# The first nine attention units as one flat list, and batch 1's values by casting DMA

## The chip, the cores and the metric

The kernel runs on one core of a Trainium2 chip. Its engines are TensorE (PE in the profile; PEld is its weight loads), VectorE (DVE), ScalarE (ACT), GpSimd (POOL) and SyncE (SP, which here only issues DMAs). Each takes its instructions in the order of the program and waits on semaphores for the others. The metric is the device time of one execution, in microseconds (us).

## The reference

Two stages, the second fed by the first:

```python
# attention: B=8 batches, H=8 heads, 512 local and 32 global positions, head size 64
k_all = concat([k_g, k_l]);  v_all = concat([v_g, v_l])
out_g = softmax(scale * q_g @ k_all.T) @ v_all               # global queries see everything
s_ll  = where(|i - j| <= 32, scale * q_l @ k_l.T, -1e9)      # local queries: a window
out_l = softmax(concat([scale * q_l @ k_g.T, s_ll])) @ v_all # and the global keys
x = concat([out_g, out_l]) reshaped to (4352, 512)
# mixture of E=8 experts, F=1024
P = exp(x @ w_gate - max);  8 times: P /= rows' sums; P /= columns' sums; P *= N / E
out = sum over e of P[:, e] * (relu(x @ w1[e]) @ w2[e])
```

## The kernel before, in words

**Units.** Attention is cut into 32 units: unit n is two heads (pair n mod 4) of batch n // 4. A unit goes through these steps, each a function:

- st_A (L266): TensorE transposes keys and queries (fp16, cast before by POOL, cast_qk) into PSUM; VectorE copies the keys to kTe, ACT the queries to the block-diagonal qbd (two copies).
- st_B0 and st_B (L314, L287), in three parts: scores of eight blocks of 64 queries against a window of 128 keys and the 32 global keys; row minima or maxima on VectorE, exp with its sums on ACT into Pu. Batch 0 uses st_B0 (mask added by TensorE), the others st_B (mask added by VectorE).
- st_N (L343): reciprocals and scaling of Pu on VectorE, the global part Pl on POOL.
- st_D1, st_D2 (L355, L363): transposes of Pu and Pl and their copies out of PSUM, pw on VectorE, pg on ACT.
- st_E (L371): weights times values into po, copied to xT, the first layer's input. The first layer of batch 0 needs st_E of units 0 to 3.

The global queries have steps of their own, st_G0, st_G1, st_GN, st_G2 and st_G3, for a half batch each; transpose_g (L205) makes their keys kgT and queries qgT from what cast_g cast.

**Values.** st_E reads values of a batch in two tilings, va and vb, and global ones in vgz. From batch 2 on, load_v (L174) fetches them with POOL-issued DMAs that cast fp32 to fp16; SP then copies va to vb (move_vb) and fills vgz (load_vz). Batches 0 and 1 are loaded raw in fp32 (load_vrow), cast by POOL to vsr and rearranged by TensorE with a 0/1 matrix: select_v (L151), four 128x512 matmuls into one PSUM tile and a copy, for each 128-row piece. Batch 0 takes eight such products, batch 1 five, and two DMAs from ACT's queue fill the rest of its vb.

**Fillers.** The first layer of experts 0 to 3 (p_l1, L461) is mixed into attention. One block is four 128x512 matmuls and a ReLU out of PSUM by ACT or VectorE; f1("a") or f1("v") (L490) issues the next one, in the order expert 0, 1, 2, 3 for batch 0 (eight blocks each), then batch 1, and so on. A block of a batch is let through only from slot 4 x batch + 5 on. Expert weights come by load_w1e (L477), a casting DMA that POOL issues into a software queue. What stays over of the fillers is done beside the Sinkhorn iterations after attention, and then the other experts follow.

**Order.** Nothing is scheduled by a tool: the order of calls is the order on each engine. Units 0 to 2 are emitted by a loop (L525 to L558), the next steps by straight code up to L585, units 4 on by the loop at L588, with special cases for its first rounds. From its round 9 the loop has a steady form: one unit and seven or eight fillers a round, 30 in four rounds. Fillers begin in round 4, two there and seven in each of rounds 5 to 8. DMAs on SP's queue (q, k, raw values, global keys and queries, value moves, results) are issued in the same program order.

PSUM pools: mm and sc two buffers each, po one, tr two. kTe has eight buffers, Pu, pw and pg two.

Of the kernel before, what the change touches and what calls it, by code (L numbers as in the profile page):

```python
# [23 lines left out]
def kernel(  # L24
# [67 lines left out]
    with tc.tile_pool(name="att_c", bufs=1) as att_c, \  # L92
# [42 lines left out]
        vraw = {}  # L135

        def load_vrow(b):
            shape = [P, H, NJ, Dh]
            f = vraw[b] = (hpool.tile(shape, FP32, tag="hT", name="vraw") if b else
                           wpool.tile(shape, FP32, tag="w2e", name="vraw", bufs=1))  # L140
            for g in range(2):
                nc.sync.dma_start(out=f[:, 4 * g : 4 * g + 4].rearrange("p h s d -> p h (s d)"),
                                  in_=v_l[b, 4 * g : 4 * g + 4].rearrange("h (p s) d -> p h (s d)", s=NJ))

        def cast_vrow(b, gs=(0, 1)):
            f = vraw[b]
            for g in gs:
                h = slice(4 * g, 4 * g + 4)
                nc.gpsimd.tensor_copy(out=vsr[:, :, h, :], in_=f[:, h].rearrange("p h s d -> p s h d"))

        def select_v(b, t, js, po=()):  # L151
            for j in js:
                c0 = P * j + HB * t
                pool, tag = (ps_po, "po") if j in po else (ps_mm, "mm")
                pv = pool.tile([P, D], FP32, tag=tag, name="pv")
                for so in range(NJ):
                    nc.tensor.matmul(pv, zsel[:, so, c0 : c0 + P], vsr[:, so], start=(so == 0), stop=(so == NJ - 1))
                cp = nc.vector.tensor_copy if j % 2 == 0 else nc.scalar.copy
                cp(out=vab[b % 2][t][:, j], in_=pv.rearrange("p (h d) -> p h d", h=H))
# [70 lines left out]
        load_vrow(0)  # L230
# [35 lines left out]
        def st_A(n):  # L266
# [11 lines left out]
            for a in range(2):  # L278
                r = slice(HB * a, HB * (a + 1))
                o = qb[r, :, HB * a : HB * (a + 1)].rearrange("p i (q s) -> p i q s", s=NJ)  # L280
                i = pq[r, 1, :].rearrange("p (s i q) -> p i q s", s=NJ, i=NHB)
                if b == 0:
                    nc.scalar.mul(o, i, -scale)
                else:
                    nc.scalar.copy(out=o, in_=i)  # L285
# [69 lines left out]
        def st_D1(n):  # L355
# [5 lines left out]
            nc.vector.tensor_copy(out=d["pw"], in_=ptw)  # L361

        def st_D2(n):  # L363
# [5 lines left out]
            nc.scalar.copy(out=d["pg"], in_=pt)  # L369

        def st_E(n):  # L371
# [13 lines left out]
            cp = nc.vector.tensor_copy if HP <= n < 2 * HP else nc.scalar.copy  # L385
            cp(out=xT[b][:, hp, :], in_=po)
# [138 lines left out]
        for s in range(3):  # L525
            for part in range(3):
                st_B0(s, part)
            if s >= 1:
                st_D1(s - 1)
                st_D2(s - 1)  # L530
            if s == 0:
                cast_vrow(0)
                cast_qk(0, 1, gq)
                load_qk(1, 0, (nc.sync, nc.sync))
                load_g(k_g, kgf)
                load_w1e(0)
                nc.vector.memset(qbd[1], 0.0)
            elif s == 1:
                load_vrow(1)
                load_qk(1, 1, (nc.sync, nc.sync))  # L540
                load_vg(1)
                init_vgz(vgz[1], nc.gpsimd)
                load_vz(1)
                qgf = hpool.tile([P, H, NJ * Dh], FP32, tag="hT", name="qgf")
                load_g(q_g, qgf)
            else:
                load_w1e(1)
                nc.gpsimd.dma_start(out=wg_sb, in_=moe_w_gate.rearrange("(dko dki) e -> dki dko e", dki=P))
                cast_qk(1, 0, gq)
                gk0 = cast_g(kgf, 0)  # L550
            pad_k((kTe[s + 2],))
            st_A(s + 1)
            if s < 2:
                select_v(0, s, (0, 1), (0,))
                st_N(s, 0, 6)
                if s == 0:
                    select_v(0, 0, (2, 3), (3,))
                st_N(s, 6, NHB)  # L558
        select_v(0, 1, (2, 3))
        st_B0(3, 0)  # L560
        st_B0(3, 1)
        st_E(0)
        st_A(4)
        st_B0(3, 2)
        st_N(2, 0, 6)
        st_N(2, 6, NHB)
        cast_vrow(1, (0,))
        pad_k(kTe[5:7])
        nc.vector.memset(mask[:, :, KW:SW], 0.0)
        nc.vector.tensor_scalar(out=mask[:, :, 0:KW], in0=m16, scalar1=-HUGE * 8.0, scalar2=None, op0=ALU.mult)  # L570
        st_E(1)
        st_D1(2)
        st_D2(2)
        transpose_g(gk0, 0, kgT)
        st_N(3, 0, 6)
        st_N(3, 6, NHB)
        st_B(4, 0)
        st_E(2)
        cast_vrow(1, (1,))
        load_w1e(2)  # L580
        for t in qgbd:
            nc.vector.memset(t, 0.0)
        st_D1(3)
        st_B(4, 1)
        st_D2(3)  # L585
        gat = {s: s - 5 for s in range(5, 9)}
        gat.update({2 * j + 1: j for j in range(4, NU // 2)})
        for s in range(HP, NU + 1):  # L588
# [8 lines left out]
            if s == HP:  # L597
                st_A(s + 1)
                st_B(s, 2)
                st_E(s - 1)  # L600
                st_N(s, 0, 6)
                st_N(s, 6, NHB)
                select_v(1, 0, (0, 1))
                st_B(s + 1, 0)
                select_v(1, 0, (2, 3))
                select_v(1, 1, (NJ - 1,))
                slot = s + 1
                va, vb = vab[1]
                nc.scalar.dma_start(out=vb[0:HB, 0 : NJ - 1], in_=va[HB:P, 0 : NJ - 1])
                nc.scalar.dma_start(out=vb[HB:P, 0 : NJ - 1], in_=va[0:HB, 1:NJ])  # L610
                cast_qk(1, 1, gq)
                gcast = [(cast_g(x[0], x[1]), x) for x in ((kgf, 1, kgT), (qgf, 0, qgT), (qgf, 1, qgT))]
                load_w1e(3)
            else:
                if HP + 1 < s <= 2 * HP:
                    st_B(s, 0)
                if s > 2 * HP:
                    f1("a")
                st_D1(s - 1)
                if g23:  # L620
                    st_GN(*gp)
            if g1 and s > HP + 1:
                st_G0(*gn)
            f1("a" if s > 2 * HP else "aa")
            if s > HP:
                st_D2(s - 1)
            if 2 * HP < s < NU:
                st_B(s, 0)
            if g23 and s <= 2 * HP:
                st_G2(*gp)  # L630
            if HP < s < NU:
                st_B(s, 1)
            if s > HP:
                f1("vv" if g23 else "va")
            if g23 and s > 2 * HP:
                st_G2(*gp)
            if HP < s < NU - 1:
                st_A(s + 1)
            if HP < s < NU:
                st_B(s, 2)  # L640
            if s > HP:
                f1("v")
                st_E(s - 1)
# [4 lines left out]
            if g23:  # L648
                st_G3(*gp)
# [589 lines left out]
```

## Time and profile before

| | before |
|---|---|
| median of 3 runs | 1031.53 us (1030.57 to 1031.58) |
| the profiled execution | 1031.69 us, its span 1029.9 us |
| first filler block starts | 46.17 us |
| round 9 starts | 91.83 us |
| granted TensorE clock, mean | 0.997 |

In the table of stretches, a row holds the stretch in us from the span's start, its length, and for PE, PEld, DVE, ACT and POOL the busy time with the number of instructions in brackets; then the granted TensorE clock, the mean busy share of the 16 DMA engines, and GB/s. In a row of a group of instructions stand line, engine, operation, output<-inputs, shapes and count; after the first bar the busy time in us and the mean ns of one; after the second the idle time just before them and what ended it. A row of the timeline begins with its start and its length in us. "us min/median/max" at a DMA is from its issue to its landing; the rows named q0 are the software queue's packets, MB and share of 16 engines.

### The profile page before, as it was taken

What the parts mean: (1) busy time and instruction counts of PE and PEld (TensorE: products, weight loads), DVE (VectorE), ACT (ScalarE), POOL (GpSimd) and SP (SyncE); (2) the same over time, 40 slices, a digit from 0 to 9 for tenths busy, and PEclk for the clock granted to TensorE, in tenths of its full rate; (3) what the DMA queues carried; (4) which work ended last, traced back from release to release, by engine and by line L of the source; (5) the groups of instructions that cost most, each with busy time, mean ns of one, the idle gap of its engine ahead of it and who ended that gap; (6) DMA issues with size and microseconds to landing.
All of it is one profiled execution on the core that took longest, in us unless ns stands there. A gap on an engine that the chain in (4) does not pass through costs nothing.

```text
span 1029.9 us, 23231 instructions
## 1 busy us (share of the span) xinstructions
PE 1004.5 (98%) x9286; PEld 741.1 (72%) x9286; DVE 891.1 (87%) x1740; ACT 528.7 (51%) x1328; POOL 172.2 (17%) x265
## 2 busy tenths in 40 slices
PE   7899999999999999999999999999999999999998
PEld 4555555555555466777778878878878878888887
DVE  8688877877775768999879999999999999999995
ACT  7767888888886674222223434333333333433431
POOL 7341423414403003021110000000000000000000
PEclk9899999999999999999999999999999999999999
DMA  9896698989946989957646656665755746746750
GB/s 269 192 221 194 135 277 203 218 238 205 222 144 173 285 283 308 310 182 279 235 159 232 200 188 230 200 191 193 224 186 184 240 175 206 232 173 194 220 195 27
DMA packets 103180, 216.87 MB, mean 211 GB/s; under 512 B 34384, under 2 KB 67616, under 8 KB 92576
## 3 DMA queue, kind: packets, MB, share of 16 engines
q1 hardware_dynamic: 52576, 165.38, 46.4%
q0 software_dynamic: 47888, 40.39, 21.9%
q10 hardware_dynamic: 2608, 9.64, 2.4%
q8 instruction: 72, 1.18, 0.5%
q14 instruction: 36, 0.29, 0.1%
HBM read 174.41 MB, written 59.12 MB: 227 GB/s over the span
## 4 chain that ended last, share of the span: by engine, by line
PE 83%; DVE 8%; ACT 6%; issue 2%; DMA 1%; SPq 0%; POOL 0%; ACTq 0%; DVEq 0%
PE m L931 27%; PE ph L468 18%; PE ph L820 11%; PE pm L931 10%; PE pf L838 10%; ACT Pu L311 2%; DVE Pu L348 2%; DVE h L693 1%; ACT qbd L285 1%; PE ptw L359 1%; PE pt L275 1%; DVE s L693 1%; PE po L380 1%; ACT hT L471 1%; DMA vraw<-in_v_l_dram 1%
## 5 line engine op out<-in xcount | busy, mean ns | idle before, releaser
L468 PE MATMUL ph<-xT,w1e 128*128 128x512 f16 (+1 forms) x1152 | 259.7, 367 | 2.7 <-ACT hT L471 1.3
L931 PEld LDWEIGHTS <-h 128*128 128x128 f16 x2160 | 209.9, 98 | 35.7 <-DVE h L693 2.2
L931 PE MATMUL m<-w2c,s 128*128 128x256 f16 x1620 | 199.9, 273 | 0.0
L931 PEld LDWEIGHTS <-s 128*128 128x128 f16 x1620 | 158.5, 98 | 26.6
L468 PEld LDWEIGHTS <-w1e 128*128 128x128 f16 x1152 | 105.1, 98 | 98.0 <-issue 8.8
L822 ACT ACTIVATE h<-ph 128x512 f16<-128x512 f32 (+1 forms) x144 | 79.1, 550 | 150.2 <-PE ph L820 140.9
L693 DVE TENSOR_TENSOR h<-h,pb 128x2048 f16<-128x2048 f16 (+2 forms) x66 | 154.9, 2347 | 0.5 <-DMA h<-hd 0.5
L845 ACT ACTIVATE h<-pf 128x512 f16<-128x512 f32 x144 | 82.1, 596 | 123.4 <-PE pf L838 112.0
L693 DVE TENSOR_TENSOR s<-h 128x1024 f16<-128x1024 f16 (+2 forms) x178 | 127.5, 757 | 17.4 <-ACT h L822 12.8
L931 PE MATMUL m<-w2c,h 128*128 128x256 f16 x1080 | 138.2, 273 | 0.0
L820 PE MATMUL ph<-xs,w1s 128*128 128x512 f16 (+1 forms) x576 | 127.3, 355 | 0.0
L931 PE MATMUL pm<-w2c,h 128*128 128x256 f16 x1080 | 124.8, 273 | 0.5
L471 ACT ACTIVATE hT<-ph 128x512 f16<-128x512 f32 (+1 forms) x188 | 102.1, 559 | 38.1 <-PE ph L468 36.0
L838 PEld LDWEIGHTS <-w1q 128*128 128x128 f16 x1008 | 98.6, 98 | 11.4
L311 ACT ACTIVATE Pu<-ms,mx 128x160 f16<-128x160 f32 x224 | 93.3, 424 | 4.6 <-DVE mx L308 3.9
L473 DVE TENSOR_SCALAR hT<-ph 128x512 f16<-128x512 f32 x100 | 67.7, 686 | 28.2 <-PE ph L468 28.0
L693 DVE TENSOR_TENSOR h<-h 128x1024 f16<-128x1024 f16 (+1 forms) x178 | 91.5, 555 | 0.4
L693 DVE TENSOR_TENSOR xs<-xg,pb 128x1024 f16<-128x1024 f16 (+2 forms) x48 | 79.7, 1661 | 7.9 <-DMA hd<-hT 7.8
L820 PEld LDWEIGHTS <-w1s 128*128 128x128 f16 x576 | 56.4, 98 | 37.7
L838 PE MATMUL pf<-xs,w1q 128*128 128x256 f16 x576 | 80.5, 273 | 0.0
L308 DVE CUSTOM_DVE_ANT_0 ms<-sc,mask 128x160 f32<-128x160 f32 x224 | 59.2, 318 | 9.6 <-PE sc L303 9.5
L838 PE MATMUL pf<-t,w1q 128*128 128x256 f16 x432 | 64.8, 273 | 0.0
(168 smaller groups left out, 1217.5 us busy)
## 6 DMA issues: line engine op xcount, KB each, us to landing
h<-hd SPq DMA_DIRECT2D x32, 1024.0 KB
w1q<-w1c SPq DMA_DIRECT2D x36, 896.0 KB
hd<-hT SPq DMA_DIRECT2D x26, 1024.0 KB
w1s<-w1d SPq DMA_DIRECT2D x18, 1024.0 KB
pb<-pd SPq DMA_DIRECT2D x64, 256.0 KB
w2c<-in_moe_w_dram POOLq DMA_DIRECT2D x16, 512.0 KB, 22.3
out_dram<-o POOLq DMA_DIRECT2D x8, 1024.0 KB, 4.7
f<-in_q_l_dram SPq DMA_DIRECT2D x15, 512.0 KB
```

The lines of the kernel that those rows point to most:

```text
L308: nc.vector.tensor_tensor_reduce(out=ms[:, ii, :], in0=sc[:, SW * ii : SW * (ii + 1)], in1=mask[:, mi, :], scale=-scale, scalar=BIG, op0=A ...
L311: nc.scalar.activation(out=d["Pu"][:, i, :], in_=ms[:, ii, :], func=AF.Exp, scale=-1.0, bias=d["mx"][:, i : i + 1], accum_out=d["sm"][:, i ...
L348: nc.vector.tensor_tensor(out=d["Pu"][:, i0:i1, 0:KW], in0=d["Pu"][:, i0:i1, 0:KW], in1=d["rs"][:, i0:i1].unsqueeze(2).to_broadcast([P, i1 ...
L468: nc.tensor.matmul(ph[:, 0:n], wts[e][:, dk, P * fm : P * (fm + 1)], xT[m][:, dk, :], start=(dk == 0), stop=(dk == DP - 1))
L471: nc.scalar.activation(out=hT[:, fm, 0:n], in_=ph[:, 0:n], func=AF.Relu)
L473: nc.vector.tensor_scalar(out=hT[:, fm, 0:n], in0=ph[:, 0:n], scalar1=0.0, scalar2=None, op0=ALU.max)
L693: nc.vector.tensor_tensor(out=out, in0=in0, in1=in1, op=op)
L820: nc.tensor.matmul(ph[:, 0:n], w1s[i][:, dk, P * fm : P * (fm + 1)], xss[i][:, dk, 0:n], start=(dk == 0), stop=(dk == DP - 1))
L822: nc.scalar.activation(out=hs[i][:, fm, 0:n], in_=ph[:, 0:n], func=AF.Relu)
L838: nc.tensor.matmul(bank[:, 256 * c : 256 * (c + 1)], self.w[:, self.sta[q], k, P * c : P * (c + 1)], self.mov[q][:, k], start=(first and c ...
L845: nc.scalar.activation(out=self.h[:, k : k + 2, 256 * c : 256 * (c + 1)], in_=bank.rearrange("p (k t) -> p k t", k=2), func=AF.Relu)
L931: nc.tensor.matmul(pm[:, HD * t : HD * (t + 1)], lhs[0][:, k, lhs[1] + P * t : lhs[1] + P * (t + 1)], w[:, k, q - 1, :], start=(k == 0 and ...
```

## The change

The loop over units 0 to 2, the straight code and the loop's rounds 4 to 8 are replaced by one flat list of calls for units 0 to 8; the loop begins at round 9, in its steady form. In the list the parts of different units are interleaved singly, and fillers stand as single blocks between other steps; there are 30 of them, as before.

- Batch 1's values: load_vrow, cast_vrow and the five select_v of batch 1 go; load_v(1) is called instead, with a memset of 32 rows of va that it leaves unwritten. Batch 0 keeps its eight products, in another order.
- st_A, st_D1, st_D2, st_E and select_v take the engine of their copies as an argument ("a" ACT, "v" VectorE). So pw of units 1, 2, 4 and 5 is copied by ACT, qbd of unit 5 by VectorE, pg of units 5 and 7 by VectorE, xT of unit 1 and 6 by VectorE and of the other units by ACT.
- The expert weights are issued in the order 1, 2, 0 ahead of the fillers and 3 after the eighteenth of them; before, 0, 1, 2, 3.
- Loads of q, k and global keys and queries, their casts, paddings and clears stand at other places of the list.

```diff
-        def load_vrow(b):
-            shape = [P, H, NJ, Dh]
-            f = vraw[b] = (hpool.tile(shape, FP32, tag="hT", name="vraw") if b else
-                           wpool.tile(shape, FP32, tag="w2e", name="vraw", bufs=1))
+        vraw = wpool.tile([P, H, NJ, Dh], FP32, tag="w2e", name="vraw", bufs=1)
...
-        def select_v(b, t, js, po=()):
...
-                cp = nc.vector.tensor_copy if j % 2 == 0 else nc.scalar.copy
...
+        def copy(eng, out, in_):
+            (nc.scalar.copy if eng == "a" else nc.vector.tensor_copy)(out=out, in_=in_)
+        def select_v(t, j, eng, po):
...
-        def st_A(n):
+        def st_A(n, eng="a"):
...
-        def st_D1(n):
+        def st_D1(n, eng="v"):
...
-            nc.vector.tensor_copy(out=d["pw"], in_=ptw)
+            copy(eng, d["pw"], ptw)
...
-        def st_D2(n):
+        def st_D2(n, eng="a"):
...
-        def st_E(n):
+        def st_E(n, eng="a"):
...
-            cp = nc.vector.tensor_copy if HP <= n < 2 * HP else nc.scalar.copy
-            cp(out=xT[b][:, hp, :], in_=po)
+            copy(eng, xT[b][:, hp, :], po)
...
-        for s in range(3):
-            for part in range(3):
-                st_B0(s, part)
-            if s >= 1:
...
+        st_B0(0, 0)
+        cast_vrow()
+        nc.vector.memset(qbd[1], 0.0)
+        st_A(1, "a")
+        cast_qk(0, 1, gq)
+        st_B0(0, 1)
+        pad_k((kTe[4],))
+        st_B0(0, 2)
+        st_B0(1, 0)
+        st_N(0, 0, 6)
+        pad_k((kTe[2],))
+        st_N(0, 6, NHB)
+        select_v(1, 1, "a", 0)
+        load_qk(1, 0, (nc.sync, nc.sync))
+        st_B0(1, 1)
+        pad_k((kTe[6],))
+        load_g(k_g, kgf)
+        st_D1(0, "v")
+        select_v(1, 3, "v", 1)
+        load_qk(1, 1, (nc.sync, nc.sync))
+        st_B0(1, 2)
+        st_A(2, "a")
+        st_N(1, 0, 6)
+        pad_k((kTe[3],))
+        pad_k((kTe[5],))
+        load_w1e(1)
+        select_v(0, 3, "a", 1)
+        st_N(1, 6, NHB)
+        cast_qk(1, 0, gq)
+        st_D2(0, "a")
+        select_v(0, 0, "a", 0)
+        load_w1e(2)
+        st_B0(2, 0)
+        gk0 = cast_g(kgf, 0)
+        st_B0(2, 1)
+        st_A(3, "a")
+        select_v(1, 0, "v", 0)
+        st_D1(1, "a")
+        load_w1e(0)
+        st_B0(2, 2)
+        select_v(0, 2, "v", 1)
+        st_N(2, 0, 6)
+        init_vgz(vgz[1], nc.gpsimd)
+        select_v(0, 1, "a", 0)
+        st_D2(1, "a")
+        qgf = hpool.tile([P, H, NJ * Dh], FP32, tag="hT", name="qgf")
+        load_g(q_g, qgf)
+        st_B0(3, 0)
+        st_A(4, "a")
+        st_N(2, 6, NHB)
+        select_v(1, 2, "v", 1)
+        nc.gpsimd.dma_start(out=wg_sb, in_=moe_w_gate.rearrange("(dko dki) e -> dki dko e", dki=P))
+        st_B0(3, 1)
+        st_B0(3, 2)
+        st_E(0, "a")
+        vq = load_v(1)
+        run(vq[:3])
+        st_D1(2, "a")
+        run(vq[3:])
+        g0 = cast_g(kgf, 1)
+        st_D2(2, "a")
+        cast_qk(1, 1, gq)
+        st_E(1, "v")
+        st_B(4, 1)
+        st_B(4, 2)
+        st_D1(3, "v")
+        st_A(5, "v")
+        st_E(2, "a")
+        st_N(4, 0, 6)
+        g1_ = cast_g(qgf, 0)
+        st_D2(3, "a")
+        g2_ = cast_g(qgf, 1)
+        st_E(3, "a")
+        st_B(5, 0)
+        transpose_g(g1_, 0, qgT)
+        slot = HP + 1
+        f1("a")
+        load_qk(2, 0, (nc.sync, nc.sync))
+        st_B(5, 1)
+        f1("v")
+        transpose_g(g0, 1, kgT)
+        transpose_g(g2_, 1, qgT)
+        f1("a")
+        f1("a")
+        nc.gpsimd.memset(vab[1][0][0:W, 0], 0.0)
+        st_N(4, 6, NHB)
+        st_B(5, 2)
+        f1("v")
+        st_A(6, "a")
+        f1("v")
+        st_G0(0, 1)
+        st_G0(0, 0)
+        st_D1(4, "a")
+        st_G1(0, 0)
+        f1("v")
+        f1("v")
+        st_D2(4, "a")
+        vq = load_v(2)
+        run(vq[:3])
+        load_qk(2, 1, (nc.sync, nc.sync))
+        st_B(6, 0)
+        st_N(5, 0, 6)
+        f1("v")
+        st_E(4, "a")
+        f1("a")
+        st_B(6, 1)
+        st_A(7, "a")
+        logits(0, NJ)
+        st_G1(0, 1)
+        cast_qk(2, 0, gq)
+        f1("v")
+        f1("a")
+        st_N(5, 6, NHB)
+        st_B(6, 2)
+        f1("v")
+        f1("a")
+        st_GN(0, 0)
+        st_D2(5, "v")
+        st_D1(5, "a")
+        f1("v")
+        f1("a")
+        f1("a")
+        st_N(6, 0, 6)
+        st_B(7, 0)
+        st_GN(0, 1)
+        st_G0(1, 0)
+        f1("a")
+        st_A(8, "a")
+        load_w1e(3)
+        f1("a")
+        st_G2(0, 0)
+        st_N(6, 6, NHB)
+        st_B(7, 1)
+        st_G1(1, 0)
+        f1("v")
+        st_B(7, 2)
+        st_D1(6, "v")
+        f1("v")
+        f1("v")
+        st_G3(0, 0)
+        st_G2(0, 1)
+        st_E(5, "a")
+        cast_qk(2, 1, gq)
+        f1("a")
+        f1("a")
+        st_D2(6, "a")
+        st_N(7, 0, 6)
+        st_N(7, 6, NHB)
+        st_B(8, 0)
+        st_GN(1, 0)
+        load_qk(3, 0, (nc.sync, nc.sync))
+        st_G3(0, 1)
+        st_G0(1, 1)
+        f1("v")
+        st_E(6, "v")
+        st_G2(1, 0)
+        st_D2(7, "v")
+        run(vq[3:])
+        f1("a")
+        st_B(8, 1)
+        f1("v")
+        st_D1(7, "v")
+        f1("a")
+        st_G1(1, 1)
+        st_B(8, 2)
+        st_N(8, 0, 6)
+        st_N(8, 6, NHB)
+        f1("a")
+        load_qk(3, 1, (nc.sync, nc.sync))
+        f1("a")
+        st_E(7, "a")
+        st_A(9, "a")
+        st_G3(1, 0)
+        gat = {8: 3, **{2 * j + 1: j for j in range(4, NU // 2)}}
+        for s in range(2 * HP + 1, NU + 1):
...
```

More of the change, by code (lines that the diff above doesn't have):

```diff
@@ L610 @@
[L610 to L623, printed above, removed]
```

154 lines of the change are left out of this document (42 added, 112 removed).

## The prediction

> **What bounds the kernel now.** I read the page's first part, then the table of busy time by stretch, then idle time by group of instructions in the stretches that the change rewrites, and last the DMA issues.
>
> ```profile
> span 1029.9 us, 23231 instructions
> PE 1004.5 (98%) x9286; PEld 741.1 (72%) x9286; DVE 891.1 (87%) x1740; ACT 528.7 (51%) x1328; POOL 172.2 (17%) x265
> ```
>
> TensorE is busy for 98% of the span, so time comes back only where it stands still or does work that goes away. The edit ends where the loop takes over at unit 9. The three rows below cut the beginning at two events: the first filler block (its matmuls start at 46.17 us) and unit 9 (91.83 us); both rows follow the table, and the third row is one whole batch of the loop.
>
> ```profile
> core 0: us, PE busy (x) PEld busy (x) DVE busy (x) ACT busy (x) POOL busy (x), PEclk, DMA share, GB/s
> 8.40:46.17 37.77, 28.38 (x386) 19.79 (x386) 29.71 (x85) 29.81 (x111) 21.12 (x23) 0.91 1.01 233
> 46.17:91.83 45.66, 42.27 (x488) 24.58 (x487) 35.69 (x115) 31.92 (x101) 17.01 (x33) 1.00 0.72 169
> 91.83:131.20 39.37, 38.37 (x457) 22.75 (x455) 32.20 (x115) 32.89 (x107) 13.22 (x22) 1.00 0.75 201
> ...
> 46.17 1.89 PE L468 MATMUL ph<-xT,w1e 128*128 128x512 f16 x8
> ...
> 91.83 1.02 PE L468 MATMUL ph<-xT,w1e 128*128 128x512 f16 x4
> ```
>
> In the first stretch nothing is full: ACT 29.81 and DVE 29.71 of 37.77 us, 79% each. In the second TensorE shows 42.27 of 45.66, but that flatters it: a matmul counts until its modelled end, so a waiting block still looks busy. The batch of the loop is the better measure: the code gives it the same 30 filler blocks (7+8+7+8 in its four units, against 2+7+7+7+7 before unit 9) and four units of attention, and it takes 39.37 us. The second stretch is 6.3 us longer for nearly the same work.
>
> What the engines wait for in the first stretch:
>
> ```profile
> L340 ACT ACTIVATE Pu<-sc,mx 128x160 f16<-128x160 f32 x32 | 12.1, 403 | 3.2 <-DVE mx L336 3.2
> L311 ACT ACTIVATE Pu<-ms,mx 128x160 f16<-128x160 f32 x11 | 4.6, 418 | 3.8 <-DVE mx L308 3.7
> ...
> L159 ACT CAST va<-pv 128x512 f16<-128x512 f32 x4 | 2.3, 586 | 0.6 <-PE pv L157 0.6
> L386 ACT CAST xT<-po 128x512 f16<-128x512 f32 x4 | 2.3, 586 | 0.0
> L285 ACT COPY qbd<-pt 64x512 f16<-64x512 f16 x4 | 2.3, 586 | 0.1
> ...
> L369 ACT COPY pg<-pt 128x256 f16<-128x256 f16 x4 | 1.6, 392 | 0.0
> ```
>
> ACT waits 6.9 us for row maxima that VectorE makes late, because whole steps of a unit stand in a row and each engine runs its queue in order. That is a fault of order, not of capacity.
>
> **The change part by part.**
>
> Batch 1's selecting products. Five of the thirteen go (20 of the 52 matmuls below).
>
> ```profile
> L157 PE MATMUL pv<-vsr,zsel 128*128 128x512 f16 x52 | 12.4, 378 | 1.6 <-POOL vsr L149 0.7 <-DVE va L159 0.6 <-ACT Pu L340 0.4
> ...
> 43.72 2.61 PE L157 MATMUL pv<-vsr,zsel 128*128 128x512 f16 x11
> ...
> L149 POOL CAST vsr<-vraw 128x1024 f16<-128x1024 f32 x4 | 4.1, 1035 | 0.8 <-DMA vraw<-in_v_l_dram 0.8
> ```
>
> Eleven in 2.61 us, the last one's drain included, is about 0.22 us each: 4.4 us of TensorE. As TensorE isn't what fills that stretch, I count the removal only where the copies fall on the full engines: two of ACT's (2 x 0.586 = 1.2 us; a third lies past the cut) and two of VectorE's (rows below, 2 x 0.69 = 1.4). The 1 MB load of raw values and two of the four casts on POOL (1.035 us each) go too; POOL is 21.12 of 37.77 us busy there, so I count nothing for them.
>
> Copies that change engine before the first filler: D1 of units 1 and 2 move from VectorE to ACT; E of unit 1 and both qbd copies of unit 5 move from ACT to VectorE.
>
> ```profile
> L159 DVE CAST va<-pv 128x512 f16<-128x512 f32 x4 | 2.7, 686 | 0.4 <-PE pv L157 0.4
> L361 DVE COPY pw<-ptw 128x1024 f16<-128x1024 f16 x4 | 2.7, 673 | 0.6 <-PE ptw L359 0.6
> ...
> L430 ACT COPY pgs<-pt 128x640 f16<-128x640 f16 x3 | 2.1, 709 | 0.0
> ```
>
> No row shows the 1024-wide copy on ACT. Its 256-wide copy takes 0.392 and its 640-wide 0.709 us, 0.83 ns an element, so 1.03 us is my estimate (bounds 0.709 and 2 x 0.709). VectorE's qbd copies I take at ACT's 0.59 each. ACT: 29.81 - 1.2 - 0.59 - 1.17 + 2.06 = 28.9 us. VectorE: 29.71 - 1.4 - 2 x 0.67 + 0.69 + 1.17 = 28.8.
>
> The interleaving. In the list a unit's parts no longer stand together: two parts of unit 2, the keys of unit 3 and a product share a stretch, so ACT always has an exp whose maximum is made. Bounds for the time in which 28.9 us of work pass: at today's 79%, 36.6 us; at 95%, 30.4. The loop's batch has ACT at 32.89/39.37 = 84% while TensorE is the full engine. I take 88%, between these: 32.8 us. First filler at 8.4 + 32.8 = 41.2 us, bounds 38.8 and 45.0. Gain 5.0 us.
>
> The weights' order. POOL now issues expert 1's weights, then 2's, then 0's, and the first filler needs expert 0's. These are casting DMAs on one software queue.
>
> ```profile
> 13.54 0.78 POOL L481 DMA_DIRECT2D w1e<-in_moe_w_dram  x1
> ...
> 15.17 0.84 POOL L352 TENSOR_TENSOR Pl<-Pu,rs 128x256 f16<-128x256 f16 x1 [0.85 <-DVE rs L347]
> ...
> 21.16 0.86 POOL L352 TENSOR_TENSOR Pl<-Pu,rs 128x256 f16<-128x256 f16 x1 [2.77 <-DVE rs L347]
> 21.96 0.81 POOL L481 DMA_DIRECT2D w1e<-in_moe_w_dram  x1
> ...
> DMA to landing us min/median/max: 10.3/11.9/12.9
> ...
> q0 software_dynamic: 524, 0.93, 82.7%
> ...
> q0 software_dynamic: 341, 0.70, 95.7%
> ```
>
> The last two rows are that queue in 26:32 us beside other loads (0.155 MB/us) and in 40:44 nearly alone (0.175 MB/us): a 1 MB tile takes 5.7 to 6.5 us of a queue that is never empty. On POOL the first issue now stands behind Pl of unit 0 (ends at 16.0 today), the second behind Pl of unit 1 (22.0) and two casts of 1.04, the third behind one more cast and the second's 0.81: 16, 24 and 26 us by today's times. The first lands like today's slowest (12.9 later, 28.9); the queue is then not empty, and the others follow 5.7 to 6.5 us apart: about 34.7 and 40.5. So the weights come just ahead of the first filler and cost nothing by this reckoning; with the cover gone, each us that they are later costs one. At a full 11.9 us each they would land at 16 + 3 x 11.9 = 51.7 (a rival).
>
> Batch 1's values by casting DMA. Batch 2's show the price:
>
> ```profile
> 71.84 0.80 POOL L181 DMA_DIRECT2D va<-in_v_l_dram  x1
> 72.63 1.79 POOL L184 DMA_DIRECT2D va<-in_v_l_dram  x2
> ...
> va<-in_v_l_dram POOLq DMA_DIRECT2D x1, 128.0 KB, 3.5
> vb<-in_v_l_dram POOLq DMA_DIRECT2D x1, 32.0 KB, 2.8
> ...
> 86.01 0.50 SPq L171 DMA_DIRECT2D vb<-va  x1
> 86.56 0.59 SPq L172 DMA_DIRECT2D vb<-va  x1
> 87.24 2.07 SPq L166 DMA_DIRECT2D vgz<-vg  x4
> ...
> DMA packets 1987, 0.26 MB, mean 129 GB/s; under 512 B 1986, under 2 KB 1986, under 8 KB 1986
> ```
>
> The last row is 74:76 us: half of one batch's 0.5 MB in 2 us, all in packets under 512 B, so 4 us of queue. Queued behind the weights they land at about 45.5; SP then copies to vb and fills vgz, 3.3 us of issue and about 2.8 to land: 51.6 us. The reader is E of unit 4, which stands behind nine fillers. At the loop's pace (39.37 / 30 = 1.31 us a filler with its attention) that is 41.2 + 11.8 = 53.0. Cost 0, with 1.4 us to spare; bounds 0 and +4. Behind the waiting copies on SP stand xd of batch 0 and batch 2's q and k, read much later.
>
> The Trainium skill speaks against such a load: "DMA: Bandwidth & Descriptors", Specifications, says that transfers under 512 B are read-modify-write and miss line rate. The 2 us row agrees; the term above is taken from that row.
>
> Second stretch, first filler to unit 9. The list has the same 30 blocks, each alone between attention steps, and the loop's order begins with all its state as before. Floor: the loop's 39.4; the three transposes for global keys and queries left in it today are partly moved up, so they add under 1 us. ACT receives D1 of units 4 and 5, VectorE gives those and E of units 4, 5 and 7: at 31.92 and 35.69 both have room. Bounds 39.4 and today's 45.66. I take 42.3, half of the excess kept, as a start has batch-1 and batch-2 loads running that the loop has behind it. Gain 3.4 us.
>
> Sum: unit 9 at 41.2 + 42.3 = 83.5 instead of 91.83 us: -8.3. From there the program and the blocks left are the same.
>
> ```profile
> 340.00:360.00 20.00, 20.00 (x102) 9.55 (x101) 15.81 (x45) 13.14 (x22) 0.00 (x0) 1.00 1.14 278
> ...
> 600.00:800.00 200.00, 199.75 (x1733) 168.75 (x1732) 190.22 (x256) 76.52 (x134) 7.54 (x8) 1.00 0.61 200
> ```
>
> These rows show TensorE full later too, so nothing waits there for a fixed time and the shift should arrive whole (bounds: all of it, or none where a late load sets the pace). The profiled execution took 1031.69 us (span 1029.9 and 1.79 around it), 0.16 above the median of 1031.53; 1031.69 - 8.3 = 1023.4, and I leave the 0.16 out.
>
> **The rivals.**
>
> 1. Only the first stretch packs (13%). The single blocks meet two PSUM buffers; if ACT or VectorE frees them late, the second stretch stays at 45.66: 1031.69 - 5.0 = 1026.7. For it: one slow copy holds the next block. Against: the loop does it at 39.4.
>
> 2. Expert 0's weights come late and TensorE's clock falls (16%).
>
> ```profile
> 28.00:31.00 3.00, 1.17 (x37) 1.09 (x31) 2.60 (x6) 2.98 (x14) 0.00 (x0) 1.00 1.12 239
> 31.00:38.00 7.00, 5.83 (x104) 5.00 (x104) 5.59 (x25) 3.69 (x14) 3.55 (x5) 0.51 0.82 187
> ```
>
> After 3 us in which TensorE worked 1.17, the granted clock was 0.51 for 7 us. Today that falls on attention; a wait of 4 us in front of the fillers would put it on dense matmuls, where half a clock for 7 us costs up to 3.5. With the first filler at 45.2 and 3 us for the clock: 45.2 + 3 + 42.3 = 90.5, or 1030.4, no difference that shows. The Trainium skill, "TensorE: Matmul & The Clock Gate", Part 1, would have the clock halve after an idle window of about 3.4 us; the rows above fell after less idling than that.
>
> 3. Slower (15%): the software queue is the bound. If three weight tiles pass at today's 11.9 us each, fillers begin at 51.7, batch 1's values follow at 62.8 (11.1 later, as above) just as E of unit 4 wants them, and the slow clock costs 3: 51.7 + 42.3 + 3 = 97.0, +5.2, 1036.9. It decides once expert 0's weights land after 91.83 - 42.3 - 3 = 46.5 us, that is if a tile takes over 10.2 us. For it: the landing times. Against: two issues 8.4 us apart overlapped in today's queue, and its rate is nearer 6 us a tile.
>
> The forecast has the rest, 56%.
>
> **How the numbers follow.** Forecast 1023.4; its own range 1019 to 1027, from the first filler 2 us either way and the second stretch 39.9 to 44. The lowest ends of both stretches (38.8 + 39.9 = 78.7, -13.1) give 1018.6. The range runs from there to 1032.0, over rivals 1 and 2, and leaves out rival 3 and some 5% below. A measurement of this kernel can tell about 0.2%, 2.1 us. Faster: forecast 56, rival 1 13 and the better half of rival 2's spread 6, 75%; same: the other 10%; slower 15%.
>
> **What would show it.** The first filler between 39 and 45 us with no long TensorE idle ended by the weights' DMA; ACT and DVE near 88% busy in the stretch before it; unit 9 between 80 and 87 us; E of unit 4 waiting under 2 us; the granted clock at 1.0 once fillers run. Wrong: a gap above 3 us ahead of the first filler, or a second stretch over 45 us, or unit 9 early and the end not early by as much.

## The result, and the profile after

| | before | after |
|---|---|---|
| median of the runs | 1031.55 us (1030.57 to 1032.69, 12 runs) | 1028.43 us (1025.37 to 1030.20, 12 runs) |
| the profiled execution | 1031.69 us, span 1029.9 | 1029.59 us, span 1027.8 |
| first filler starts | 46.17 us | 46.92 us |
| unit 9 starts | 91.83 us | 90.01 us |

The changed kernel takes 0.9969 of the time (95% interval 0.9960 to 0.9978): 3.1 us less, where 8.1 were forecast. In the profiled execution 2.1 us are gained, and 1.8 of them are there when unit 9 starts. The first filler, forecast 5 us earlier, starts 0.75 us later than before; what is gained comes from the second stretch (43.09 us from first filler to unit 9, against 45.66 before).

The page of the changed kernel:

```profile
span 1027.8 us, 23198 instructions
PE 999.8 (97%) x9266; PEld 738.5 (72%) x9266; DVE 889.7 (87%) x1735; ACT 530.2 (52%) x1328; POOL 175.1 (17%) x269
```

TensorE has 4.7 us less to do, the five products, and stands still for 2.6 us more than before (28.0 of the span against 25.4). Its table of busy time by stretch, cut at the same events as before, and then the first stretch cut once more:

```profile
8.40:46.92 38.52, 23.01 (x368) 16.55 (x366) 30.04 (x82) 28.61 (x108) 24.29 (x27) 0.88 1.11 212
46.92:90.01 43.09, 42.55 (x481) 24.70 (x480) 35.13 (x117) 33.54 (x101) 16.68 (x34) 0.95 0.93 214
90.01:129.40 39.39, 38.93 (x460) 23.01 (x457) 31.61 (x114) 34.53 (x111) 12.97 (x22) 1.00 0.68 169
...
8.40:38.00 29.60, 20.62 (x322) 14.65 (x319) 26.48 (x74) 26.30 (x100) 21.02 (x24) 0.99 1.13 240
38.00:46.92 8.92, 2.39 (x48) 1.90 (x47) 3.56 (x9) 2.30 (x8) 3.26 (x4) 0.50 1.04 120
46.92:50.70 3.78, 3.78 (x16) 1.44 (x14) 1.51 (x7) 1.57 (x6) 0.86 (x2) 0.50 0.52 88
```

Up to 38 us the list packs as hoped: ACT is busy for 26.30 of 29.60 us and VectorE for 26.48, 89% each. Then little works for nearly 9 us: TensorE is busy for 2.39 of 8.92 us, at half the clock, and ACT for 2.30. The groups of the first stretch say the same of the order (line, engine, operation, shapes, count; busy and mean ns; idle time before and its releaser):

```profile
L339 ACT ACTIVATE Pu<-sc,mx 128x160 f16<-128x160 f32 x32 | 12.2, 401 | 1.2 <-DVE mx L335 1.0
L310 ACT ACTIVATE Pu<-ms,mx 128x160 f16<-128x160 f32 x11 | 4.6, 446 | 0.9 <-DVE mx L307 0.9
L148 ACT COPY pw<-ptw 128x1024 f16<-128x1024 f16 x2 | 2.1, 1032 | 0.0
```

ACT's waits for row maxima fell from 6.9 to 1.9 us. What stands still at the end is seen in the timeline, TensorE first, then POOL and SP's queue (start, length, in brackets the idle time before it and its releaser):

```profile
37.74 0.40 PE L366 MATMUL pt<-identity,Pl 128*128 128x128 f16 x2 [3.43 <-POOL Pl L351]
46.39 0.60 PE L207 MATMUL pt<-identity,gs 64*128 64x64 f16 x8 [6.21 <-POOL gs L199]
46.92 1.89 PE L466 MATMUL ph<-xT,w1e 128*128 128x512 f16 x4
...
35.48 0.59 POOL L184 DMA_DIRECT2D vb<-in_v_l_dram  x1 [1.99 <-DMA w1e<-in_moe_w_dram]
37.06 0.62 POOL L351 TENSOR_TENSOR Pl<-Pu,rs 128x256 f16<-128x256 f16 x1
45.30 2.02 POOL L199 CAST gs<-qgf 64x1024 f16<-64x1024 f32 x2 [5.66 <-DMA qgf<-in_q_g_dram]
...
18.54 19.03 SPq L194 DMA_DIRECT2D qgf<-in_q_g_dram  x8
```

The first filler has its weights, but in front of it in TensorE's queue stands transpose_g(g1_, 0, qgT), the transpose of the global queries. It waits 6.21 us for POOL's cast, and the cast waits for the eight DMAs that fetch the queries. SP began to issue these at 18.54 and was done at 37.57; they were all in at 45.3. A second wait, 3.43 us, stands ahead of it: POOL stood still for 1.99 us, until a weight tile had landed, before it issued the next value DMA, and Pl of unit 3 is behind that DMA and a cast on POOL.

Before, the same casts waited for the same load too, for 3.79 us, and it cost nothing at the first filler. The timeline of the kernel before, POOL and TensorE:

```profile
50.06 2.02 POOL L202 CAST gs<-qgf 64x1024 f16<-64x1024 f32 x2 [3.79 <-DMA qgf<-in_q_g_dram]
...
54.43 0.79 PE L210 MATMUL pt<-identity,gs 64*128 64x64 f16 x16
```

There the queries came in at 50 us, and their transposes stood behind the first fillers, which begin at 46.17. The list moved a reader of that load ahead of the first filler.

Why the load is late: the DMA queues of the changed kernel from 28 to 32 us (packets, MB, share of 16 engines), and two pieces of its chain of waits:

```profile
q0 software_dynamic: 366, 0.73, 96.9%
q1 hardware_dynamic: 149, 0.14, 13.3%
...
16.77 13.61 DMA f<-in_q_l_dram
...
30.40 13.98 DMA qgf<-in_q_g_dram
```

POOL's casting DMAs (three weight tiles, then batch 1's values) hold the engines, and what SP issued beside them gets 0.14 MB in 4 us: 512 KB of q take 13.6 us, a 64 KB piece of the queries 14.0. The Trainium skill, "DMA: Bandwidth & Descriptors", Queues, rings and completion order, has each engine take turns between queues by whole packets; by the rows the software queue got 2.5 packets to one of SP's, and seven times the engine time. Whether SP's queue always had one ready, and whether the page's packets are those of the profile, no row shows.

### The profile page after: what moved, and what is told of

Same layout as the page of the kernel before. It is cut to its first block, busy times and chain, and to the rows that moved or that the text cites. A ratio compares the mean times of both kernels' runs of the same rounds, so it can differ in the third digit from the quotient of the medians.

```text
span 1027.8 us, 23198 instructions
## 1 busy us (share of the span) xinstructions
PE 999.8 (97%) x9266; PEld 738.5 (72%) x9266; DVE 889.7 (87%) x1735; ACT 530.2 (52%) x1328; POOL 175.1 (17%) x269
## 4 chain that ended last, share of the span: by engine, by line
PE 85%; DVE 5%; ACT 4%; DMA 3%; issue 1%; POOL 0%; SPq 0%; DVEq 0%; POOLq 0%; ACTq 0%
PE m L1016 27%; PE ph L466 19%; PE ph L905 11%; PE pm L1016 10%; PE pf L923 10%; ACT Pu L310 2%; DMA qgf<-in_q_g_dram 1%; DMA f<-in_q_l_dram 1%; DVE h L778 1%; PE ptw L358 1%; DVE Pu L347 1%; PE pt L272 1%; PE po L379 1%; PE sc L300 1%; DVE s L778 1%
## 5 line engine op out<-in xcount | busy, mean ns | idle before, releaser
L466 PE MATMUL ph<-xT,w1e 128*128 128x512 f16 (+1 forms) x1152 | 262.5, 368 | 2.3 <-ACT hT L469 0.9
L469 ACT ACTIVATE hT<-ph 128x512 f16<-128x512 f32 (+1 forms) x189 | 103.0, 559 | 43.4 <-PE ph L466 41.2
## 6 DMA issues: line engine op xcount, KB each, us to landing
w2c<-in_moe_w_dram POOLq DMA_DIRECT2D x16, 512.0 KB, 23.6
```

The source lines that it names most:

```text
L466: nc.tensor.matmul(ph[:, 0:n], wts[e][:, dk, P * fm : P * (fm + 1)], xT[m][:, dk, :], start=(dk == 0), stop=(dk == DP - 1))
L469: nc.scalar.activation(out=hT[:, fm, 0:n], in_=ph[:, 0:n], func=AF.Relu)
```

## The experiments

All of them are edits of the changed kernel but the fourth, which edits the kernel before. The table has, from each one's profiled execution, the start of the first filler and of unit 9; then medians with their runs, and the ratio to before with its 95% interval. The kernels before that ran beside them had medians of 1031.42 to 1031.59. The two starts are each of one execution. The twelve runs of after spread over 4.8 us (before: 2.1), so a start that is 2 or 3 us earlier, as in w0_first or warm, can be of the execution and not of the edit; what a trace names as the wait, and the medians, are the firmer evidence.

| kernel | first filler | unit 9 | profiled | median (runs) | ratio |
|---|---|---|---|---|---|
| after | 46.92 | 90.01 | 1029.59 | 1028.43 (12) | 0.9969 (0.9960 to 0.9978) |
| w2_late | 38.63 | 82.06 | 1021.63 | 1023.61 (4) | 0.9928 (0.9912 to 0.9943) |
| tr_late | 42.18 | 87.2 | 1026.80 | 1026.64 (4) | 0.9956 (0.9941 to 0.9971) |
| w0_first | 43.78 | 86.9 | 1026.55 | 1028.25 (9) | 0.9973 (0.9963 to 0.9983) |
| v_cast_alone | 43.61 | 90.53 | 1030.43 | 1029.26 (10) | 0.9982 (0.9973 to 0.9992) |
| qg_first | 42.52 | 86.04 | 1025.65 | 1025.36 (4) | 0.9939 (0.9925 to 0.9954) |
| sp_split | 46.07 | 88.87 | 1029.12 | 1028.61 (8) | 0.9971 (0.9958 to 0.9983) |
| sel_list | 44.05 | 91.67 | 1031.08 | 1033.45 (10) | 1.0021 (1.0010 to 1.0033) |
| warm | 44.00 | 84.50 | 1024.12 | 1025.30 (6) | 0.9945 (0.9927 to 0.9963) |
| w12_late | 40.92 | 83.02 | 1022.53 | 1020.98 (4) | 0.9899 (0.9885 to 0.9914) |
| w12_warm | 39.74 | 82.03 | 1023.17 | 1022.22 (4) | 0.9911 (0.9894 to 0.9928) |

### One weight tile out of the start: w2_late

```diff
         select_v(0, 0, "a", 0)
-        load_w1e(2)
         st_B0(2, 0)
...
         nc.gpsimd.memset(vab[1][0][0:W, 0], 0.0)
+        load_w1e(2)
```

> The changed kernel with expert 2's weights issued after the fourth filler instead of ahead of them. Theory Q (in the changed kernel the first filler, at 46.9 us, stands behind the transposes of the global queries, whose loads land at 45.3 because three weight tiles and batch 1's values fill the DMA engines): with one tile less the global queries land by 38 to 40, the first filler starts at 41 to 42.5, unit 9 at 84 to 86.5 instead of 90.0, and the time is 3.5 to 6 us below the changed kernel. Theory W (the fillers wait for expert 0's weights, because they come third): they come second, so it gains too, 4 to 6 us; this run does not tell Q from W, the next two do. Theory L (the list itself paces the start, no load does): no change within 1 us.

Measured: 1023.61 us, 4.8 less than after. Its timeline (TensorE, SP's queue), its queues from 28 to 32 us, and its second stretch:

```profile
38.63 1.04 PE L466 MATMUL ph<-xT,w1e 128*128 128x512 f16 x4
...
82.06 1.03 PE L466 MATMUL ph<-xT,w1e 128*128 128x512 f16 x4
...
18.02 10.65 SPq L194 DMA_DIRECT2D qgf<-in_q_g_dram  x8
...
q0 software_dynamic: 301, 0.62, 82.3%
q1 hardware_dynamic: 273, 0.25, 29.9%
...
38.63:82.06 43.43, 41.29 (x482) 24.43 (x480) 36.38 (x126) 34.74 (x107) 18.32 (x35) 1.00 1.08 240
```

With one megabyte less in the software queue SP's loads get 0.25 MB in these 4 us instead of 0.14, the queries are issued in 10.65 us instead of 19.03, and the filler starts 8.3 us earlier, at full clock (1.04 us a block instead of 1.89). That is 2.4 us earlier than theory Q expected. So a less crowded queue brings the queries in earlier, and the list itself is good for a first filler ahead of the 41.2 us forecast. Expert 0's weights come second here too, so the queries are told from the weights only by the next two runs. The execution shown is the fastest of the four, whose median is 2 us above it.

### The transpose of the queries behind four fillers: tr_late

```diff
-        transpose_g(g1_, 0, qgT)
         slot = HP + 1
...
         transpose_g(g0, 1, kgT)
+        f1("a")
+        f1("a")
+        transpose_g(g1_, 0, qgT)
         transpose_g(g2_, 1, qgT)
-        f1("a")
-        f1("a")
```

> The changed kernel with the first transpose of the global queries moved behind the fourth filler, loads unchanged. Theory Q: the first filler no longer stands behind the global queries and starts when expert 0's weights are there, at 42.4 to 43 us instead of 46.9; unit 9 comes 2 to 4 us earlier and so does the end. Theory W: the weights end the wait anyway, the first filler moves by under 0.5 us and the time by under 0.5.

Measured: 1026.64 us, 1.8 less than after, just under what was expected. Its timeline and its stretches around the first filler:

```profile
42.18 1.89 PE L466 MATMUL ph<-xT,w1e 128*128 128x512 f16 x4 [1.89 <-DMA w1e<-in_moe_w_dram]
...
38.00:42.18 4.18, 1.96 (x41) 1.46 (x39) 2.69 (x9) 2.30 (x8) 2.38 (x2) 0.50 1.27 166
42.18:46.00 3.82, 3.82 (x14) 1.43 (x14) 0.82 (x6) 1.62 (x6) 0.66 (x1) 0.50 1.00 99
```

With the queries out of the way, the filler waits for expert 0's weights, the third tile in the software queue, until 42.2 us, and starts at half clock. So the queries were the last wait, and the weights are the next, 4.7 us before it.

### Expert 0's weights first: w0_first

```diff
-        load_w1e(1)
+        load_w1e(0)
...
-        load_w1e(2)
+        load_w1e(1)
...
-        load_w1e(0)
+        load_w1e(2)
```

> The changed kernel with the weights issued in the order 0, 1, 2 at the same three places. Theory W: expert 0's weights land 14 us earlier, the first filler moves from 46.9 to about 41, the time falls by 4 to 6 us. Theory Q: the bytes ahead of the global queries are the same, so the first filler stays at 46 to 47.5 and the time within 1 us of the changed kernel.

Measured: 1028.25 us, 0.2 less than after, no difference. Its timeline:

```profile
43.24 0.60 PE L207 MATMUL pt<-identity,gs 64*128 64x64 f16 x8 [4.00 <-POOL gs L199]
43.78 1.46 PE L466 MATMUL ph<-xT,w1e 128*128 128x512 f16 x3
```

The queries are still what ends last, and the filler follows them. In this execution it starts 3.1 us earlier than in after, where theory Q expected it unmoved; but this is among the fastest of its nine runs, 1.7 us under their median, and the median did not move. The weights' order alone does not hold the start.

### The casting DMA of the values alone, in the kernel before: v_cast_alone

```diff
-                load_vrow(1)
                 load_qk(1, 1, (nc.sync, nc.sync))
-                load_vg(1)
                 init_vgz(vgz[1], nc.gpsimd)
-                load_vz(1)
+                run(load_v(1))
+                nc.gpsimd.memset(vab[1][0][0:W, 0], 0.0)
...
-        cast_vrow(1, (0,))
...
-                select_v(1, 0, (0, 1))
```

The rest of batch 1's casts, products and copies goes too.

> The kernel before with one part of the change alone: batch 1's values by casting DMA, issued where the raw values were loaded; its five selecting products, their copies and the two DMAs after them are gone. If the removed 4.4 us of TensorE work lie on the path there: first filler at 42 to 43 us instead of 46.2 and 2.5 to 4 us below the kernel before. If loads set the pace of the start (theory Q carried over: global queries land at 50 us in the kernel before and are wanted at 54): the fillers start earlier but unit 9 gains under 1.5 us.

Measured: 1029.26 us, 2.3 less than before (0.1% to 0.3%). Its first filler:

```profile
43.61 0.81 PE L468 MATMUL ph<-xT,w1e 128*128 128x512 f16 x3
```

The filler comes 2.6 us earlier than the 46.17 of before, and half of that is lost again in a second stretch of 46.9 us instead of 45.66: unit 9 gains 1.3 us, as expected if loads set the pace.

### The list with the products back: sel_list

```diff
-        vq = load_v(1)
-        run(vq[:3])
...
+        for t, j, eng in ((0, 0, "v"), (0, 1, "a"), (0, 2, "v"), (0, 3, "a"), (1, 3, "v")):
+            select_v(t, j, eng, 0, 1)
```

The raw load stands behind the global queries on SP, its two casts behind theirs on POOL, and the five products behind the fourth filler.

> The changed kernel with one part undone: batch 1's values loaded raw behind the global queries and rearranged by five selecting products, placed behind the fourth filler. If the part is worth its removed TensorE work: 3 to 4.5 us above the changed kernel. If its small-packet DMAs, which take the engines from 36 to 40 us while the last global queries wait, cost what it saves: the first filler at 42 to 44 instead of 46.9, 4.4 us of products given back, and the time within 1.5 us of the changed kernel.

Measured: 1033.45 us, 5.0 more than after, above what either branch expected, and 1.9 more than before. Its timeline and its second stretch:

```profile
50.13 4.64 PE L155 MATMUL pv<-vsr,zsel 128*128 128x512 f16 x20
...
44.05:91.67 47.62, 46.96 (x502) 26.43 (x501) 36.44 (x120) 34.89 (x103) 18.88 (x35) 0.96 0.82 192
```

Beside fillers the five products cost what TensorE needs for them, 4.64 us: the second stretch is 4.5 us longer than after's 43.09. The list does not pay without the casting DMA, at least with the products at that place, and each of the two parts alone is worth little or less than nothing; 2.3 us less and 1.9 more do not add to the 3.1 of both.

### The queries earlier on SP's queue: qg_first

```diff
         load_g(k_g, kgf)
+        qgf = hpool.tile([P, H, NJ * Dh], FP32, tag="hT", name="qgf")
+        load_g(q_g, qgf)
         st_D1(0, "v")
...
-        load_g(q_g, qgf)
...
-        cast_qk(1, 1, gq)
         st_E(1, "v")
...
         g2_ = cast_g(qgf, 1)
+        cast_qk(1, 1, gq)
```

> The changed kernel with the loads of the global queries issued ahead of those of batch 1's second half of q and k, and their casts ahead of that half's casts; the same bytes. Theory O (order on SP: the last of eight global-query DMAs goes out at 37.3 us only because it is held until the q and k ahead of it have landed): the global queries land by 28 to 34, the first filler starts when expert 0's weights land, 42 to 43, and the time is 1.5 to 3.5 us below the changed kernel, unless unit 6 then waits for its own q and k. Theory B (the engines are full, whatever the order): they land after 40, the first filler is at 44 or later and the time within 1 us.

Measured: 1025.36 us, 3.1 less than after. Its timeline, SP's queue and TensorE:

```profile
16.58 7.00 SPq L194 DMA_DIRECT2D qgf<-in_q_g_dram  x8
...
42.52 1.89 PE L466 MATMUL ph<-xT,w1e 128*128 128x512 f16 x4 [0.36 <-DMA w1e<-in_moe_w_dram]
```

Issued from 16.6 to 23.6, ahead of batch 1's second q and k, the queries pass, and again the weights are next, at 42.5. Their casts, at 39.09, wait for no load. No byte was taken off the queues, so theory B falls: what made the queries late in after was the crowd together with their place, behind 1 MB of q and k on SP's own queue, which the crowd had slowed.

### Is it a semaphore on SP? sp_split

In the built program the DMAs that SP issues use eight completion semaphores in turn, so each is held until the eighth before it has landed. In after the seventh and eighth load of queries were so held by batch 1's slow q and k: SP's waits there are 0.9 us for q, until 30.4, and 6.2 us for k, until 37.3. Here two loads of queries go earlier, and none of the other six is the eighth behind those.

```diff
+        load_g(q_g, qgf, range(2))
         load_g(k_g, kgf)
...
-        load_g(q_g, qgf)
+        load_g(q_g, qgf, range(2, B))
```

> Of the changed kernel two of the eight loads of global queries are issued earlier, directly ahead of the loads of global keys; the other six stay where they are, behind batch 1's second q and k. The DMAs on SP's queue take eight completion semaphores in turn, so in the changed kernel the seventh and the eighth load of global queries waited until that q and k had landed (30.4 and about 37.3 us), and the seventh landed at 44.4. Now no load of global queries is the eighth behind that q or k. Theory S (the wait for a completion semaphore is what makes the queries late): the six issues pass in a row, over by 22 us, and the casts no longer wait for the queries at the end of the stretch; expert 0's weights, landing at about 42.4, are next, so the first filler starts at 42 to 44 instead of 46.92, and the time is 2 to 4 us below the changed kernel's 1028.4. Theory C (the crowded DMA engines alone make them late, whenever they are issued): the queries still land at 43 us or later, the first filler at 46 to 47, and the time within 1 us of the changed kernel's.

Measured: 1028.61 us, 0.2 more than after. Its timeline (SP's queue, TensorE) and two pieces of its chain of waits:

```profile
20.00 12.27 SPq L194 DMA_DIRECT2D qgf<-in_q_g_dram  x6
...
46.07 1.89 PE L466 MATMUL ph<-xT,w1e 128*128 128x512 f16 x4
...
20.85 4.85 SPq L194
...
29.19 14.37 DMA qgf<-in_q_g_dram
```

Theory S falls. Without that wait six issues still take 12.27 us, and what is issued at 29.2 lands 14.4 us later, as in after. The semaphore is not the cause; it only passes the lateness on. The six loads stand behind the same q and k as in after, beside the same crowd. Why an issue itself takes so long then is not settled by these runs.

### The clock: warm

Sixteen 128x512 matmuls that nothing reads, no part of the computation, stand ahead of the transpose.

```diff
+        wm = ps_mm.tile([P, Sl], FP32, tag="mm", name="wm")
+        for i in range(16):
+            nc.tensor.matmul(wm, identity, kTe[0][:, W : W + Sl], start=True, stop=True)
         transpose_g(g1_, 0, qgT)
```

> The changed kernel with 16 extra 128x512 matmuls into an unread PSUM tile in the place where TensorE waits for the global queries (40.2 to 46.4 us there, the clock at 0.50 from 38 to about 50). Theory K (the slow clock after the wait costs time of its own): TensorE is busy in the wait, the fillers start at 46.5 to 47.5 as before but at clock 1.0, unit 9 comes 1 to 2.2 us earlier and the time is 1 to 2 us below the changed kernel. Rival (only the wait counts, the second stretch is paced by ACT and VectorE anyway): within 0.5 us.

Measured: 1025.30 us, 3.1 less than after, in six runs that spread from 1023.79 to 1029.46. Its second stretch:

```profile
44.00:84.50 40.50, 40.37 (x482) 24.02 (x480) 34.48 (x117) 33.55 (x101) 17.53 (x34) 1.00 1.00 230
```

The clock is at 1.00 from the first filler on, and the stretch is 2.6 us shorter than after's 43.09. The rest of this execution's gain is its first filler, at 44.00 instead of 46.92, as the queries came earlier; the edit does not explain that.

### Weights in the order of need: w12_late, and warm again: w12_warm

```diff
-        load_w1e(1)
+        load_w1e(0)
...
-        load_w1e(2)
...
-        load_w1e(0)
...
         run(vq[3:])
+        load_w1e(1)
...
         nc.gpsimd.memset(vab[1][0][0:W, 0], 0.0)
+        load_w1e(2)
```

> The run with expert 2's weights late, and besides expert 0's weights first and expert 1's behind batch 1's values. Theory Q: nothing is left to wait for at the first filler, which comes at 37.5 to 39, and the wait of 0.6 us for batch 1's global values at unit 4's E goes; the time is 0 to 1.5 us below that run (1022 to 1023.6). If expert 1's weights are now late for the ninth filler: a wait of TensorE there and 0 to 3 us above it.

Measured: 1020.98 us, 7.4 less than after and 10.6 less than before, the best median of all, 2.6 below w2_late where up to 1.5 were expected. Yet in the executions profiled its first filler, at 40.92, is later than expected and 2.3 us behind w2_late's, and it ends 0.9 us later: w2_late's is the fastest of its four, this one the slowest, so how much the second edit adds is not settled. Its casts of the queries wait for no load any more. Its second stretch, and the 4 us in which its clock had fallen:

```profile
40.92:83.02 42.10, 41.98 (x481) 24.51 (x480) 35.13 (x123) 34.88 (x107) 18.12 (x35) 0.96 1.09 252
...
34.00:38.00 4.00, 3.18 (x54) 2.92 (x54) 4.00 (x21) 3.44 (x16) 4.00 (x6) 0.50 1.87 159
```

As the clock fell here too, w12_warm adds ten unread matmuls to it, six ahead of st_E(1, "v") and four ahead of st_B(4, 2).

> The kernel with expert 0's weights first and the weights of experts 1 and 2 issued late (1020.98 us, first filler at 40.92, unit 9 at 83.02), with ten 128x512 matmuls that nothing reads: six ahead of E of unit 1 and four ahead of the last score part of unit 4. They add 2.6 us of TensorE work at full clock which is no part of the computation, in a stretch where TensorE stood still for 1.54 and 0.94 us. Theory K (the clock at 0.50 from 34 to 44.5 us is a cost of its own): the granted clock stays near 1 through 34 to 45, the first filler starts at 39 to 40.5, the second stretch is 40 to 41.5, and the time is 1 to 3 us lower, 1018 to 1020. Rival (the slow clock falls where the other engines set the pace, or the added matmuls take what they give): within 0.8 us of 1021.0 or above it.

Measured: 1022.22 us (1020.38 to 1023.62), against 1020.98 (1019.89 to 1022.53) without them. Its stretch from 34 to 38 us, its first filler, and two waits later on:

```profile
34.00:38.00 4.00, 2.59 (x57) 1.94 (x55) 4.00 (x18) 3.92 (x18) 4.00 (x6) 1.00 1.74 157
...
39.74 1.04 PE L466 MATMUL ph<-xT,w1e 128*128 128x512 f16 x4
...
423.22 1.89 PE L911 MATMUL ph<-xs,w1s 128*128 128x512 f16 x8 [0.64 <-DVE o L1042]
464.04 1.03 PE L1022 MATMUL m<-w2c,h 128*128 128x256 f16 x8 [0.66 <-DVE o L1042]
```

The clock stays at 1.00, the filler starts 1.2 us and unit 9 1.0 us earlier, and the time is not better: the two spreads of four runs overlap. In this execution 1.3 us are given back where VectorE's adding into o holds TensorE; in w12_late's TensorE had no wait between 400 and 480 us. So theory K holds for the start, and no gain in time is shown.

## Why the prediction was right or wrong

**Right: the direction, and the packing.** ACT and VectorE were put at 88% up to the first filler; they are at 89% up to 38 us, and then wait, which makes 74% and 78% of the whole stretch. Their work was put at 28.9 and 28.8 us; it is 28.61 and 30.04. The 1024-wide copy on ACT, estimated at 1.03 us, takes 1.032. ACT's waits for maxima went. Where the loads allow it, the first filler starts at 38.63 (w2_late) and 40.92 (w12_late), around and ahead of the 41.2 forecast.

**Wrong: "First filler at 41.2".** It is 46.92, 5.7 us later. The step that failed is the sentence on the second stretch, that the transposes for global keys and queries "are partly moved up, so they add under 1 us". It priced their TensorE work. It did not ask what they wait for, and the row that told it, POOL's cast waiting for the queries until 50.06, was in the trace of before and has no part in the prediction. So the 32.8 us ahead of the first filler were worked out from ACT's and VectorE's work alone, and what ended last was a load. The sign it gave for being wrong, a gap above 3 us ahead of the first filler, is there: 3.43 and 6.21 us. That the time still came out lower owes nothing to the first stretch, which was to gain 5.0 us and lost 0.75: the second gave 2.57 of its 3.4. "Cost nothing" for the weights' order had the same gap: the landing was worked out, and what the queue does to loads of other queues was not. The issues to landing of the three tiles, each in the window of its issue, were these:

```profile
w1e<-in_moe_w_dram POOLq DMA_DIRECT2D x1, 1024.0 KB, 13.4
w1e<-in_moe_w_dram POOLq DMA_DIRECT2D x1, 1024.0 KB, 13.4
w1e<-in_moe_w_dram POOLq DMA_DIRECT2D x1, 1024.0 KB, 16.8
```

Issued at 15.09, 21.77 and 25.61, they landed at about 28.5, 35.2 and 42.4, against 28.9, 34.7 and 40.5 forecast. That sum was good to 2 us; but at 42.4 the weights would have passed 41.2 too, and tr_late shows them as the next limit.

**Second stretch, 42.3.** It took 43.09, in the bounds. The 0.8 and more is the clock: 0.50 in the first 3.78 us of fillers, which the forecast had at 1.0. With the clock at 1.00 it took 40.50 in warm, but 42.29 in w12_warm and 43.43 in w2_late, where fillers begin earlier. In w2_late TensorE waits there 0.56 us for batch 1's global values and 1.08 us for POOL, which had waited 5.9 us for batch 2's q; so part of an early start's excess goes with loads, as assumed, and the rest is not taken apart.

**Batch 1's values.** E of unit 4 waits for nothing, as forecast: it stands behind late fillers, at 59.6 us. (The forecast's 45.5 for their landing is 1 us more than its 40.5 and 4 us of queue; nothing hung on it.) Counting the five products only through the copies holds only while TensorE is not full; beside fillers they are worth their whole 4.6 us (sel_list).

**The shift arrives whole.** Against before, after gains 1.82 us at unit 9 and 2.10 at the end, w2_late 9.77 and 10.06. Of the eleven kernels ten agree within 0.5 us; w12_warm lost 1.3.

**The rivals.** By its mechanism the result is nearest to rival 2, a late start and a fallen clock, though by another load than it named; its 1030.4 is 0.8 from the profiled 1029.59. By the median of 1028.43 alone rival 1's 1026.7 would be as near, which is chance. Rival 3 needed weights that land after 46.5; they did at 42.4. Rival 1 kept the first stretch's gain and lost the second's; the stretches went the other way.

The sum, corrected: 46.92 instead of 41.2 is 5.7 us, 43.09 instead of 42.3 is 0.8, together 6.5; 8.3 forecast less 6.5 is the 1.8 us measured at unit 9.

## What to carry to other kernels

When a list is reordered, follow each moved reader back to its load and read in the trace of before when that load landed: a wait that was hidden behind other work moves with its reader. Issue bulk loads in the order and at the time of their need; a tile that is fetched early for later takes the DMA engines from small loads that are needed now. Here, putting two weight tiles off, with expert 0's first, was worth 7.4 us on top of the list; the whole reordering without it was worth 3.1.

## What the runs showed of the hardware

- Beside a busy software queue (96.9% of the engines' time from 28 to 32 us) loads that SP issued got 13.3%, and a 64 KB load took 14 us to land; in sp_split one issue on SP's queue, with no wait named, lasted 4.85 us.
- The granted clock fell to 0.50 without a long idle time. In w12_late TensorE's longest wait between 31 and 35 us was 1.54 us, and it fell at 34 (0.52 from 34 to 35):

```profile
32.85 0.22 PE L379 MATMUL po<-pw,va 128*64 128x64 f16 x2 [1.54 <-ACT xT L148]
34.82 0.29 PE L300 MATMUL sc<-kTe,qbd 128*128 128x128 f16 x1 [0.94 <-DVE mx L307]
34.00:35.00 1.00, 0.18 (x3) 0.18 (x4) 1.00 (x8) 0.63 (x3) 1.00 (x2) 0.52 2.38 153
```

The Trainium skill, "TensorE: Matmul & The Clock Gate", Part 1, has it fall after an idle window of about 3.4 us; after's fall at 38, behind a wait of 3.43 us, agrees, w12_late's does not if the window must be wholly idle. Ten unread matmuls, 1.46 and 1.02 us of work (w12_warm), kept it at 1.00.
- Keeping the clock up is not the same as being faster: at half clock, from 34 to 38 us, VectorE and POOL were busy for all 4.00 us of w12_late, and the 1.0 us that full clock gave at unit 9 did not show in the time.
